# Block products for the cross terms in the second and third token groups of a GFNet + S2-MLP kernel on one Trainium2 core

## Chip, cores, metric

One core of a Trainium2 chip runs the kernel in one launch. The metric is device time in microseconds (us). The kernel before took 409.92 us, the median of three runs (409.81 to 409.93).

Engines, as the profile names them: PE (matrix products, with PEld for its weight loads), DVE (VectorE), ACT (ScalarE), POOL (GpSimd), SP (issues all transfers). Each runs its instructions in the order in which they stand in its queue, and waits there for semaphores.

## What is computed

The output is x + A(norm(x)) + B(norm(x)), for x of 2048 tokens by 448 channels:

```python
# A: spectral filter
X = rfft2(x, axes=(-2, -1))
y = irfft2(X * (w_r + 1j * w_i), s=(S, D), axes=(-2, -1))
# B: token shift, then MLP
h  = gelu(layernorm(x) @ w1)
hs = concat(shift(h[:, 0:112], +1), shift(h[:, 112:224], -1),
            shift(h[:, 224:336], +2), shift(h[:, 336:448], -2)) @ w2
x1 = x + hs
B  = x1 + gelu(layernorm(x1) @ w3) @ w4        # F = 1792 hidden channels
```

Inputs are fp32. Products run in fp16: every operand is split into a high half and a low half (the rounding rest), and a product is hi·hi + hi·lo + lo·hi.

## The kernel before

**Tiling.** The 2048 tokens are 16 blocks of 128 rows (row = 16·a + b, so a block holds every sixteenth token). The work goes through these stages, which overlap:

- layer norm of x in four groups of four blocks, `norm1`; transposes of x, partly on PE, partly as DMA transposes from SP (`turn`); w1 products (`w1_unit`, L465) and gelu; the result h goes back transposed by one DMA transpose for each block (L492) into `hT`.
- w2 products with the shifts (`w2_tile`, L510), second layer norm (`ln2`, L520), DMA transposes of its result into `x2all` (L553).
- w3 is loaded early into `w3raw` (`load_w3`, L214); its last 64 rows come once from memory and are then copied to the other 64 partitions (L1039). Sums of squares of w3 (L1043) give a power-of-two scale s3 (`powers`, with a matmul on PE at L258), and `w3_split` makes both halves.
- MLP in eight groups G = 0 to 7 of two blocks (256 tokens); a group has seven steps fp of two 128-channel slices f of the hidden layer. `front(G, fp)` (L764) makes 22 matmuls of 256 columns with w3 (L435), then the gelu on ACT (L773), the high half `hf` on ACT (L776) and the low half on DVE (L777). `back(G, fp)` (L791) multiplies by w4 into two PSUM banks `acc` (L811). `steps` (L855) interleaves them: fronts run `ahead=2` steps before backs, and cycle through the PSUM banks of `tags`, two banks to a tag.
- spectral part: `do_fold` (L571) loads x for two blocks, normalizes it on ACT and forms four sums and differences on POOL (L583, L584, L586); `step1_in` (L591) splits into halves `xh`; `step1` (L598) transforms over the rows of the block (L604). Then 16 chunks (`chunk_a`, `chunk_b`, `chunk_z`, `chunk_c`) beside G = 3 to 5, and the inverse beside G = 5 to 7.

**Block form of back.** For the groups in `STR` (G = 5, 6, 7) the cross terms hi·lo and lo·hi are not taken as whole products: the 2 × 2 blocks (two hidden slices by two token blocks for h, two slices by two column halves for w4) are multiplied in seven block products in place of eight, as in Strassen–Winograd. hi·hi stays 4 whole matmuls (L811); each of the two cross terms is 7 matmuls of 224 columns (L826). The combinations of h are made on DVE (`forms`, L786 to L788, into `hgm`), those of w4 once on POOL (`w4_forms`, L921, into `w4x`). Part of the sum lies in two more PSUM banks `cr` of tag "tr"; at the end of a group ACT copies them to `cross` (L843), and POOL (DVE for G = 7) combines (L846, L850).

**What sets the order.** A scheduler orders each engine's queue by priority and simulated readiness: `prio(EVAC)` goes first, `prio(FILL)` last. `behind(key)` pins instructions behind another on the same engine; `after[...]` keeps the keys: ("f", G, fp) is the gelu's halves, ("m", G, fp) the last matmul of a back, ("h", g, i) the transpose of h. Lists at the top pin the folds (`FOLD`, ACT behind "f"), the step1 products (`PACE`, PE behind "m"), the maxima of the spectral weights (`WMAX`, DVE, L619), and the last `ln2` (`LATE`).

**Memory that is shared.** `x2mem` holds x2all in its first 8F of 9F halves, and w4raw from 2F on to the end; `cross` is its last 896 floats and so is wsrc, and later pf_buf[1] of the chunks. The fourth buffer for folds, `xf_buf[3]`, lies in `hgm`.

Of the kernel before, what the change touches and what calls it, by code (L numbers as in the profile page):

```python
# [12 lines left out]
F32 = mybir.dt.float32  # L13
F16 = mybir.dt.float16
# [27 lines left out]

# [80 lines left out]
def body(tc, nc, x, wf, w1, w2, w3, w4, c_g, c_n, c_small, out):  # L123
# [62 lines left out]
    x2mem = pw.tile([128, 9 * F], F16, name="x2mem")  # L186
    wsrc = x2mem[:, 8 * F:8 * F + 512]
    V.memset(wsrc, 0.0)
    ones = pc.tile([128, 128], F32, name="ones")
# [36 lines left out]
    w4raw = x2mem.bitcast(F32)[:, F:].rearrange("p (f n) -> p f n", f=14)  # L226
# [293 lines left out]
    def ln2(bs, engines, pins=None):  # L520

        n, b0 = len(bs), bs[0]
        mv = stats([xb(b) for b in bs], f"b{b0}")
        a = pc.tile([128, 4], F32, tag="vb", bufs=2, name=f"vb{b0}")[:, :n]
        r = pc.tile([128, 4], F32, tag="vs", bufs=2, name=f"vs{b0}")[:, :n]
        o, y = [], []
        nm = pc.tile([128, 4], F32, tag="nm", bufs=2, name=f"nm{b0}")[:, :n]
        P.tensor_scalar(out=nm, in0=mv[:, :n, 0], scalar1=-1.0, scalar2=None, op0=ALU.mult)
        for m in range(0, n, 2):
            w = stage(f"y{b0 + m}", 8 * 448, 0 if pins else (b0 + m) // 2 % 2, F16)  # L530
            o.append(w[:, 0:4 * D].bitcast(F32).rearrange("p (i n) -> p i n", i=2))
# [12 lines left out]
        for i in range(n):
            b, h, x_ = b0 + i, y[i // 2][:, i % 2], o[i // 2][:, i % 2]
            k = r[:, i:i + 1]
            with behind("f", *pins[i]) if pins else contextlib.nullcontext():
                u = A.activation(out=h[:, 0:D], in_=x_, func=AF.Copy, scale=k)
                V.scalar_tensor_tensor(out=h[:, 448:512], in0=x_[:, 384:448], scalar=k, in1=h[:, 384:448],
                                       op0=ALU.mult, op1=ALU.subtract)  # L550
                v = V.scalar_tensor_tensor(out=h[:, 512:896], in0=x_[:, 0:384], scalar=k, in1=h[:, 0:384],
                                           op0=ALU.mult, op1=ALU.subtract)
            d = SY.dma_start_transpose(out=x2all[:, b // 4][:, :, 128 * (b % 4):128 * (b % 4) + 128], in_=h)  # L553
            after[f"b{b0}"] = u.ins, v.ins, d.ins
# [36 lines left out]
    def step1_in(b):  # L591
        f = folds.pop(b)
        t = xh_buf[b % 4]
        i = A.activation(out=t[:, 0:452], in_=f, func=AF.Copy)
        j = V.tensor_tensor(out=t[:, 452:904], in0=f, in1=t[:, 0:452], op=ALU.subtract)
        after["x", b] = i.ins, j.ins

    def step1(b):  # L598
# [192 lines left out]
    def back(G, fp):  # L791
# [47 lines left out]
        with prio(EVAC):  # L839
            if G in STR and fp == end:  # L840
                e0, e1 = cross[:, 0], cross[:, 1]
                for i in range(2):
                    A.activation(out=cross[:, i], in_=xs[G][i][:, 0:D], func=AF.Copy, scale=k34)  # L843
                for o, x, y in ((e0[:, n:], e0[:, 0:n], e0[:, n:]), (e1[:, 0:n], e1[:, 0:n], e0[:, n:]),
                                (e0[:, n:], e0[:, n:], e1[:, n:]), (e1[:, n:], e1[:, 0:n], e1[:, n:])):
                    (V if G == 7 else P).tensor_tensor(out=o, in0=x, in1=y, op=ALU.add)  # L846
            for i in range(2):
                evacuate(i)
                if G in STR and fp == end:
                    (V if G == 7 else P).tensor_tensor(out=to[i], in0=to[i], in1=cross[:, 1 - i], op=ALU.add)  # L850
                if G == 6 and fp == 6:
                    SY.dma_start(ov[:, 2 * G + i], to[i])
        yield keep(m)
# [67 lines left out]
    def w4_forms(fp):  # L921
# [4 lines left out]
        t1 = [m[:, 6], m[:, 7]]  # L926
# [7 lines left out]
        w4f[fp] += [t1] + [[x[:, i] for i in range(2)] for x in (t2, t3)]  # L934

    def squares1():
        for t in range(4):
# [165 lines left out]
    Y1 = Y.rearrange("p i q c (b k) -> p i q c b k", k=8)  # L1103
    pfd = pool("pfd", side="right")
    xf_buf = [pfd.tile([128, 2, 4, 113], F32, name=f"xf{i}") for i in range(3)]
    xf_buf.append(hgm.bitcast(F32).rearrange("p i n -> p (i n)")[:, 0:904].rearrange("p (b s d) -> p b s d", b=2, s=4))
    xh_buf = [pfd.tile([128, 2 * 452 + 16], F16, name=f"xh{i}") for i in range(4)]
    for i in range(4):
        P.memset(xh_buf[i][:, 904:], 0.0)
    mlp([1, 2], ahead=AH, tags=("mm", "tr"))  # L1110
    for b in range(0, NB, 2):
        do_fold(b)
        step1_in(b)
        step1_in(b + 1)
        with behind("m", *PACE[b // 2]):
            step1(b)
            step1(b + 1)
    with prio(FILL):
        for fp in range(7):
            with behind("fold", 0 if fp < 2 else 14):  # L1120
                w4_forms(fp)
    ln2(range(12, 16), [A] * 4, LATE)
    with behind("X", 14):
        wm = w_scale()
    close("pfd")
    with behind("m", 2, 5):
        w_scale_end(wm)
    pst = pool("pst", side="right")
    pf_buf = [pst.tile([128, 2, 2, DF], F16, name="pf0"),
# [68 lines left out]
```

## Time and profile before

| | |
|---|---|
| median of 3 runs | 409.92 us (409.81 to 409.93) |
| the profiled execution | 409.72 us |
| its span, first to last instruction | 407.6 us |
| granted PE clock | 0.999 |
| whole products of back (L811) | 508 of 448 columns, 24 of 224 |
| block products of back (L826) | 266 of 224 columns |

In the lines of the profile `out<-in` are the program's tiles, `xN` the number of instructions, then busy time and mean duration, then the idle time ahead of them with what ended it. A timeline's row starts with the start and the length in us. A row of transfers gives the size and the time from issue to landing. The row for one line of the code gives the shortest, median and longest duration in ns and the first and last start.

### The profile page before, as it was taken

The page shows a single profiled execution, that of the slowest core. Times are in us where ns is not written, and L with a number is a line of the kernel's source. Part 1 is how long each engine was busy: PE and PEld are TensorE (multiplying, and loading weights), DVE is VectorE, ACT ScalarE, POOL GpSimd, SP SyncE. Part 2 cuts the span into 40 slices and gives each one's busy share as a digit, 9 for nine tenths or more (in the row PEclk, how much of TensorE's full clock was granted, in tenths as well). Part 3 has the DMA queues.
Part 4 walks back from the last instruction along what each step waited for, and adds up shares of the span by engine and source line. Part 5 has one row for each costly group of instructions (what it writes and reads, how often), then busy time and mean ns, then how long its engine had stood idle before and what let it go on. Part 6 is the DMA issues. An engine that isn't in the chain of part 4 may idle for free.

```text
span 407.6 us, 8828 instructions
## 1 busy us (share of the span) xinstructions
PE 401.3 (98%) x3379; PEld 296.0 (73%) x3379; DVE 304.2 (75%) x658; ACT 268.6 (66%) x465; POOL 179.8 (44%) x276
## 2 busy tenths in 40 slices
PE   8998999999999999999999999999999999999996
PEld 4553555666767777776888887877788888888885
DVE  5988999899653757894577777763488879889645
ACT  4698993884737865763488888785956566544332
POOL 3889723011197747499243344441231254217100
PEclk9999999999999999999999999999999999999999
DMA  8999999915910375317055666642000022323201
GB/s 282 351 274 198 177 180 261 260 23 109 207 48 0 92 233 175 103 36 170 19 135 146 151 145 151 153 112 60 2 2 2 24 68 75 108 70 112 92 2 45
DMA packets 57209, 49.46 MB, mean 121 GB/s; under 512 B 41312, under 2 KB 52192, under 8 KB 57168
## 3 DMA queue, kind: packets, MB, share of 16 engines
q1 hardware_dynamic: 57168, 48.91, 46.4%
q8 instruction: 26, 0.43, 0.5%
q14 instruction: 15, 0.12, 0.1%
HBM read 35.06 MB, written 3.67 MB: 95 GB/s over the span
## 4 chain that ended last, share of the span: by engine, by line
PE 96%; DMA 2%; ACT 1%; DVE 0%; issue 0%; ACTq 0%
PE pw L435 33%; PE acc L811 24%; PE pw L510 9%; PE pw L465 6%; PE cr L826 4%; PE acc L826 3%; PE pu L707 3%; PE ps L604 3%; PE pp L661 2%; PE pe L727 2%; PE px L678 2%; PE py L749 2%; PE wps L889 2%; DMA h<-hs 2%; PE pta L414 1%; PE end L811 1%
## 5 line engine op out<-in xcount | busy, mean ns | idle before, releaser
L435 PE MATMUL pw<-x2mem,w3p 128*128 128x256 f16 x1232 | 149.7, 272 | 0.0
L435 PEld LDWEIGHTS <-w3p 128*128 128x128 f16 x1232 | 118.7, 98 | 19.4
L811 PE MATMUL acc<-w4p,hf 128*128 128x448 f16 x508 | 107.4, 352 | 0.0
L811 PEld LDWEIGHTS <-hf 128*128 128x128 f16 x532 | 51.5, 98 | 35.5
L777 DVE SCALAR_TENSOR_TENSOR hf<-pw,h,hf 128x512 f16<-128x512 f32 x56 | 41.8, 747 | 36.5 <-ACT hf L776 36.3
L773 ACT ACTIVATE pw<-pw,pe 128x512 f32<-128x512 f32 x56 | 36.7, 656 | 44.8 <-PE pw L435 44.6
L510 PE MATMUL pw<-w2p,h 112*128 112x448 f16 x192 | 39.2, 353 | 1.3 <-DMA h<-hs 1.2
L734 POOL TENSOR_TENSOR e<-e 128x226 f32<-128x226 f32 x16 | 11.1, 696 | 63.7 <-ACT e L731 56.2
L776 ACT ACTIVATE hf<-pw,h 128x512 f16<-128x512 f32 x56 | 38.3, 683 | 1.3
L465 PE MATMUL pw<-w1p,w4x 128*128 128x448 f16 x176 | 34.8, 352 | 0.5 <-DVE h L967 0.5
L510 PEld LDWEIGHTS <-h 112*128 112x128 f16 x192 | 18.4, 98 | 18.0 <-DMA h<-hs 2.2
L688 POOL TENSOR_TENSOR xr<-te 128x450 f32<-128x450 f32 x16 | 15.7, 981 | 34.5 <-DVE te L686 34.5
L465 PEld LDWEIGHTS <-w4x 128*128 128x128 f16 x176 | 17.1, 98 | 16.4 <-ACT w4x L424 0.7
L696 POOL TENSOR_TENSOR zb<-xr,zb 128x450 f16<-128x450 f32 x16 | 16.1, 1009 | 16.8 <-ACT zb L695 16.8
L684 DVE SCALAR_TENSOR_TENSOR te<-px,sc,wc 128x450 f32<-128x450 f32 x16 | 11.0, 685 | 10.6 <-ACT te L683 7.0
L683 ACT ACTIVATE te<-px 64x450 f32<-64x450 f32 x32 | 17.2, 538 | 1.7 <-PE px L678 1.2
L719 ACT ACTIVATE U<-y 113x512 f16<-113x512 f16 x32 | 18.0, 620 | 0.1
L741 ACT ACTIVATE vh<-e 128x448 f16<-128x448 f32 x16 | 9.2, 575 | 13.5 <-DVE e L739 13.3
L731 ACT ACTIVATE e<-pe 128x452 f32<-128x452 f32 x16 | 8.7, 545 | 14.0 <-PE pe L727 11.6
L540 POOL TENSOR_SCALAR y<-xt,nm 128x448 f32<-128x448 f32 x6 | 5.9, 986 | 23.3 <-DMA x2mem<-y 12.9
L711 DVE SCALAR_TENSOR_TENSOR y<-pu,y 113x512 f16<-113x512 f32 x16 | 10.9, 687 | 6.9 <-ACT y L710 6.8
L583 POOL TENSOR_TENSOR xr<-xf 128x452 f32<-128x452 f32 x6 | 6.7, 1125 | 20.6 <-ACT xf L579 10.5
(208 smaller groups left out, 799.0 us busy)
## 6 DMA issues: line engine op xcount, KB each, us to landing
wc<-wf SPq DMA_DIRECT2D x32, 225.0 KB, 3.8
wl<-wf SPq DMA_DIRECT2D x8, 450.0 KB, 3.9
xt<-x SPq DMA_DIRECT2D x3, 896.0 KB, 11.3
w3raw<-w SPq DMA_DIRECT2D x3, 896.0 KB, 14.6
xf<-x SPq DMA_DIRECT2D x6, 448.0 KB, 3.7
xr<-x SPq DMA_DIRECT2D x12, 224.0 KB, 2.5
out<-xr SPq DMA_DIRECT2D x12, 224.0 KB, 2.0
gn<-c_g SPq DMA_DIRECT2D x16, 128.0 KB, 3.2
```

The costliest lines, as they stand in the source:

```text
L435: m = T.matmul(ps_out, wp[:, wi + t, cols], xT[:, xi + t, tok], start=t == 0 and wi + xi == 0, stop=t == 3 and wi == 4)
L465: m = T.matmul(pm[:, :D], xTs[g][:, xi + t, 128 * i:128 * i + 128], w1p[:, wi + t], start=t == 0 and p == 0, stop=t == 3 and p == 2)
L510: m = T.matmul(w2b[b][:, :D], hT[g][:112, 4 * hi + k, o:o + 128], w2p[:, wi, k], start=k == 2 and hi + wi == 0, stop=k == 3 and hi == 1)
L683: i = A.activation(out=e[64 * h:64 * h + 64], in_=px_[64 - 64 * h:128 - 64 * h, :2 * DF], func=AF.Copy)
L688: P.tensor_tensor(out=z, in0=t[:, 0], in1=t[:, 1], op=ALU.add)
L696: P.tensor_tensor(out=zv[1], in0=z, in1=zv[0], op=ALU.subtract)
L719: A.activation(out=U[b][:113, p].rearrange("p q (c k) -> p q c k", c=NC), in_=Y1[:113, p, :, :, b], func=AF.Copy)
L773: A.activation(out=pm, in_=pm, func=AF.Gelu_apprx_tanh, scale=r3)
L776: i = A.activation(out=h[:, 0], in_=pv_, func=AF.Copy, scale=h3)
L777: j = V.scalar_tensor_tensor(out=h[:, 1], in0=pv_, scalar=h3, in1=h[:, 0], op0=ALU.mult, op1=ALU.subtract)
L811: m = T.matmul(to, h[:, hi, 2 * f + i], w4p[0][:, wi, 2 * fp + f, r], start=fp == s and f == 0 and hi + wi == 0, stop=fp == e and f == 1 a ...
L826: m = T.matmul(to, h[:, hi, slot] if slot < 4 else g[:, hi, slot - 4], w4f[fp][k][wi], start=k in (0, 6) and fp == 0 and hi == 0, stop=hi ...
```

## The change

`STR` takes in G = 1 and 2, so that `forms` and the block form of `back` run there too, and everything that stood in their way is moved:

- `w4_forms` runs on DVE (four operations a step, t1 in one), and earlier: for steps 0 to 3 behind ("f", 0, 6), for 4 to 6 behind ("f", 1, 1) to ("f", 1, 3).
- the low halves of `step1_in` run on POOL.
- fronts of G = 1 and 2 use the tag "mm" alone after the first one, since "tr" holds `cr`.
- `xf_buf[3]` moves from `hgm` to the end of `x2mem` and is used once (`FBUF`); the folds are emitted between the steps.
- the last 64 rows of w3 are loaded behind ("h", 1, 3).
- the combining at the end of groups 1 and 2 on POOL has the lowest priority.
- `PACE`, `FOLD`, `WMAX`, `LATE` change; `w_scale_end` goes behind ("m", 2, 6).

```diff
-PACE = [(0, 6), (1, 1), (1, 2), (1, 4), (1, 5), (2, 0), (2, 1), (2, 3)]
-FOLD = [(0, 5), (1, 0), (1, 1), (1, 3), (1, 4), (1, 6), (2, 0), (2, 2)]
+PACE = [(1, 0), (1, 1), (1, 2), (1, 4), (1, 5), (2, 0), (2, 1), (2, 3)]
+FOLD = [(0, 5), (0, 6), (1, 0), (1, 2), (1, 4), (1, 5), (2, 0), (2, 2)]
+FBUF = (0, 1, 2, 3, 0, 1, 2, 0)
-WMAX = [(1, 4), (1, 5), (2, 0), (2, 0), (2, 1), (2, 2), (2, 3), (2, 4)]
-LATE = [(2, 2), (2, 3), (2, 4), (2, 5)]
+WMAX = [(1, 5), (1, 6), (2, 2), (2, 3), (2, 4), (2, 4), (2, 5), (2, 5)]
+LATE = [(2, 2), (2, 3), (2, 5), (2, 6)]
-STR = (5, 6, 7)
+STR = (1, 2, 5, 6, 7)
...
-    load_w3([2, 3])
+    load_w3([2])
...
-        f = xf_buf[b0 // 2 % 4]
+        f = xf_buf[FBUF[b0 // 2]]
...
-        j = V.tensor_tensor(out=t[:, 452:904], in0=f, in1=t[:, 0:452], op=ALU.subtract)
+        j = P.tensor_tensor(out=t[:, 452:904], in0=f, in1=t[:, 0:452], op=ALU.subtract)
...
-                    (V if G == 7 else P).tensor_tensor(out=o, in0=x, in1=y, op=ALU.add)
+                with prio(EVAC if G > 2 else FILL):
+                    ...
+                        (V if G == 7 else P).tensor_tensor(out=o, in0=x, in1=y, op=ALU.add)
...
-        P.tensor_tensor(out=t3, in0=b[1][1], in1=b[0][1], op=ALU.add)
-        for i in range(2):
-            P.tensor_tensor(out=t1[i], in0=b[0][0][:, i], in1=b[0][1][:, i], op=ALU.subtract)
-            P.tensor_tensor(out=t2[:, i], in0=b[1][1][:, i], in1=t1[i], op=ALU.subtract)
-        P.tensor_tensor(out=t4, in0=b[1][0], in1=t2, op=ALU.subtract)
+        for o, x, y, op in ((t3, b[1][1], b[0][1], ALU.add), (t1, b[0][0], b[0][1], ALU.subtract),
+                            (t2, b[1][1], t1, ALU.subtract), (t4, b[1][0], t2, ALU.subtract)):
+            V.tensor_tensor(out=o, in0=x, in1=y, op=op)
...
+    with behind("h", 1, 3):
+        load_w3([3])
...
-    xf_buf.append(hgm.bitcast(F32).rearrange("p i n -> p (i n)")[:, 0:904].rearrange("p (b s d) -> p b s d", b=2, s=4))
+    xf_buf.append(x2mem.bitcast(F32)[:, 4 * F:4 * F + 904].rearrange("p (b s d) -> p b s d", b=2, s=4))
...
-    mlp([1, 2], ahead=AH, tags=("mm", "tr"))
+    gen = steps(range(1, 3), ahead=AH, tags=["tr"] + ["mm"] * 13)
+    with prio(FILL):
+        for fp in range(4):
+            with behind("f", 0, 6):
+                w4_forms(fp)
+    while ("f", 1, 3) not in after:
+        run(gen, len(slots))
+        n = len(w4f)
+        if n < 7 and ("f", 1, n - 3) in after:
+            with prio(FILL), behind("f", 1, n - 3):
+                w4_forms(n)
     for b in range(0, NB, 2):
+        while ("m", *PACE[b // 2]) not in after:
+            run(gen, len(slots))
         do_fold(b)
...
-    with prio(FILL):
-        for fp in range(7):
-            with behind("fold", 0 if fp < 2 else 14):
-                w4_forms(fp)
+    run(gen)
...
-    with behind("m", 2, 5):
+    with behind("m", 2, 6):
         w_scale_end(wm)
```

More of the change, by code (lines that the diff above doesn't have):

```diff
@@ L185, in body @@
     A.activation(out=warm, in_=warm, func=AF.Gelu_apprx_tanh)
-    x2mem = pw.tile([128, 9 * F], F16, name="x2mem")
+    x2mem = pw.tile([128, 9 * F + 16], F16, name="x2mem")
     wsrc = x2mem[:, 8 * F:8 * F + 512]
@@ L222, in body @@
     load_x(3)
-    load_w3([2, 3])
+    load_w3([2])
     cross = x2mem.bitcast(F32)[:, 4 * F:4 * F + 2 * D].rearrange("p (i n) -> p i n", i=2)
     x2all = x2mem[:, 0:8 * F].rearrange("p (j t n) -> p j t n", j=4, t=7)
-    w4raw = x2mem.bitcast(F32)[:, F:].rearrange("p (f n) -> p f n", f=14)
+    w4raw = x2mem.bitcast(F32)[:, F:9 * F // 2].rearrange("p (f n) -> p f n", f=14)
     W4F = (0, 4, 8, 11, 14)
@@ L539, in ln2 @@
                 else:
-                    e.tensor_scalar(out=o[-1][:, i], in0=xb(b0 + m + i), scalar1=1.0, scalar2=c,
-                                    op0=ALU.mult, op1=ALU.add)
+                    j = e.tensor_scalar(out=o[-1][:, i], in0=xb(b0 + m + i), scalar1=1.0, scalar2=c,
+                                        op0=ALU.mult, op1=ALU.add)
+                    after["ln", b0 + m + i] = (j.ins,)
         V.tensor_scalar(out=a, in0=mv[:, :n, 1], scalar1=eps12, scalar2=None, op0=ALU.add)
@@ L849, in back @@
                 if G in STR and fp == end:
-                    (V if G == 7 else P).tensor_tensor(out=to[i], in0=to[i], in1=cross[:, 1 - i], op=ALU.add)
+                    with prio(EVAC if G > 2 else FILL):
+                        (V if G == 7 else P).tensor_tensor(out=to[i], in0=to[i], in1=cross[:, 1 - i], op=ALU.add)
                 if G == 6 and fp == 6:
@@ L925, in w4_forms @@
         m = m.rearrange("p (k n) -> p k n", n=224)
[L926 removed]
+        t1 = m[:, 6:8]
         t2, t3, t4 = (m[:, k:k + 4:3] for k in range(3))
[L928 to L932 removed]
+        for o, x, y, op in ((t3, b[1][1], b[0][1], ALU.add), (t1, b[0][0], b[0][1], ALU.subtract),
+                            (t2, b[1][1], t1, ALU.subtract), (t4, b[1][0], t2, ALU.subtract)):
+            V.tensor_tensor(out=o, in0=x, in1=y, op=op)
         w4f[fp] = [[x[:, i] for i in range(2)] for x in (b[0][0], b[1][0], b[1][1], t4)]
[L934 removed]
+        w4f[fp] += [[x[:, i] for i in range(2)] for x in (t1, t2, t3)]
     def squares1():
```

4 lines of the change are left out of this document (2 added, 2 removed).

## The prediction

> **What bounds the kernel now.** I read the page first: the busy times, then the chain of work that ended last.
>
> ```profile
> PE 401.3 (98%) x3379; PEld 296.0 (73%) x3379; DVE 304.2 (75%) x658; ACT 268.6 (66%) x465; POOL 179.8 (44%) x276
> PE 96%; DMA 2%; ACT 1%; DVE 0%; issue 0%; ACTq 0%
> ```
>
> The span is 407.6 us and PE is busy for 401.3 of it; the chain lies on PE for 96%. Then I cut the span into stretches (busy us of PE, PEld, DVE, ACT, POOL, then clock, DMA share, GB/s).
>
> ```profile
> 0.00:32.07 32.07, 29.16 (x150) 15.55 (x151) 24.90 (x83) 20.44 (x39) 22.44 (x53) 1.00 0.99 298
> 32.07:400.00 367.93, 367.79 (x3195) 277.25 (x3196) 275.73 (x569) 246.98 (x425) 157.40 (x224) 1.00 0.43 107
> 114.20:188.70 74.50, 74.50 (x661) 56.43 (x660) 51.56 (x67) 49.49 (x88) 55.58 (x62) 1.00 0.36 103
> 301.00:370.00 69.00, 69.00 (x673) 57.91 (x672) 58.75 (x139) 38.56 (x68) 22.35 (x30) 1.00 0.18 58
> ```
>
> From 32 us to 400 us PE stands idle for 0.14 us in all, at full clock. So **less work on PE is less time**, as long as no other engine makes PE wait; and a new wait of PE anywhere there is lost one for one. Of the 2.9 us idle before 32 us, one piece matters here: PE's timeline has it just ahead of the first token mixing.
>
> ```profile
> 32.07 7.56 PE L510 MATMUL pw<-w2p,h 112*128 112x448 f16 x36 [1.17 <-DMA h<-hs]
> ```
>
> **Part 1, the products (removed from PE).** Groups 1 and 2 are 14 steps of L811, whole products: 12 matmuls of 448 columns. Groups 5 to 7 already run the block form: 4 of 448 and 14 of 224. PE's timeline of a step of each kind:
>
> ```profile
> 102.50 2.43 PE L811 MATMUL acc<-w4p,hf 128*128 128x448 f16 x12
> 104.77 2.57 PE L435 MATMUL pw<-x2mem,w3p 128*128 128x256 f16 x22
> ...
> 303.35 2.56 PE L435 MATMUL pw<-x2mem,w3p 128*128 128x256 f16 x22
> 305.75 0.92 PE L811 MATMUL acc<-w4p,hf 128*128 128x448 f16 x4
> ...
> 307.85 0.73 PE L749 MATMUL py<-vh,csm 128*128 128x448 f16 x3
> ```
>
> From start to start: whole 104.77 − 102.50 = 2.27, block 307.85 − 305.75 = 2.10. That is 0.17 saved a step, **14 × 0.17 = 2.4 us**, the largest gain in the change. The step1 products are only moved by their pins.
>
> **Part 2, the start.** Two 448 KB loads leave the first 12 us: x for the fourth fold (its buffer was hgm, free from the start; now it is the tail of x2mem, free only once w4 is split) and w3's last 64 rows (now behind the transpose of h(1,3)). DMA issues and SP's timeline:
>
> ```profile
> w3raw<-w SPq DMA_DIRECT2D x1, 448.0 KB, 18.3
> hgm<-x SPq DMA_DIRECT2D x1, 448.0 KB, 18.9
> 11.21 0.47 SPq L219 DMA_DIRECT2D w3raw<-w  x1
> 25.04 6.80 SPq L492 DMA_TRANSPOSE h<-hs  x3
> 41.57 2.66 SPq L492 DMA_TRANSPOSE h<-hs  x2
> ```
>
> The rows of w3 are issued at 11.21 and land 18.3 later, at 29.5; the x stays in flight for 18.9. The first three transposes of h meet them: 6.80 us of issue for three, against 2.66 for two later, so about 2.8 us too long. With 896 KB fewer at the 298 GB/s of that stretch the traffic ends 3.0 us sooner. PE can win at most the 1.17 us of its wait. Against that, w3's rows now come at about 44.2 (41.57 + 2.66). The nearest landing is that of their own later copy, 4.5 us; the square sums on ACT and the matmul that adds m3's sums over the partitions stand here:
>
> ```profile
> w3raw<-w3raw SPq DMA_DIRECT2D x1, 448.0 KB, 4.5
> 43.22 1.68 ACT L246 ACTIVATE xr<-w3raw 64x1792 f16<-64x1792 f32 x1
> 48.74 0.28 PE L258 MATMUL pm<-pt,ones 128*128 128x1 f32 x2
> ```
>
> 44.2 + 4.5 + 1.7 and some 0.3 for the read-out and the reduction give 50.7, so this matmul must move 2.0 us down PE's queue or PE waits 2.0; at the 18.3 of the early load it would be 15.8. Behind it wait s3 and the splits of w3 on ACT and VectorE; the copy on SP waits too, with the transposes after it. Bounds for the part: −1.2 to +2.0 (the 18.3 came at 298 GB/s of other traffic and is no guide). I take **−0.6**, half of the wait.
>
> **Part 3, VectorE in groups 1 and 2** (the stretch from 114.2 to 188.7). It loses the 16 low halves of the folds; it gains 14 × 3 forms of h and 7 × 4 forms of w4, whose durations here are (min/median/max):
>
> ```profile
> L595 DVE TENSOR_TENSOR xh<-xf,xh 128x452 f16<-128x452 f32 x12 | 11.8, 1017 | 3.1 <-ACT xh L594 3.1
> L595 DVE TENSOR_TENSOR xh<-hgm,xh 128x452 f16<-128x452 f32 x4 | 3.6, 934 | 1.0 <-ACT xh L594 1.0
> L786 DVE TENSOR_TENSOR hgm<-hf x19: 409/426/949, 291.7 to 393.0; 128x512 f16<-128x512 f16 x19
> L787 DVE TENSOR_TENSOR hgm<-hf,hgm x19: 274/283/669, 292.2 to 393.5; 128x256 f16<-128x256 f16 x19
> L788 DVE TENSOR_TENSOR hgm<-hf,hgm x19: 274/291/674, 292.5 to 393.8; 128x256 f16<-128x256 f16 x19
> ```
>
> A step's forms: 0.426 + 0.283 + 0.291 = 1.00. A form of w4 has 448 f16 elements: between the 256 of L787 (0.28) and the 512 of L786 (0.43), 0.38. So 51.56 − 15.4 + 14 × 1.00 + 28 × 0.38 = 60.8 us of 74.5. That alone fits: from 301 to 370 VectorE is at 58.75 of 69.00 and PE never waits.
>
> But these operations are held up by GpSimd. VectorE and POOL, the same low halves with POOL at work and at rest:
>
> ```profile
> 135.58 2.51 DVE L595 TENSOR_TENSOR xh<-xf,xh 128x452 f16<-128x452 f32 x2 [1.34 <-ACT xh L594]
> 135.13 1.06 POOL L583 TENSOR_TENSOR xr<-hgm 128x452 f32<-128x452 f32 x1 [0.20 <-ACT hgm L579]
> 136.15 1.45 POOL L584 TENSOR_TENSOR xr<-hgm 128x452 f32<-128x452 f32 x1
> 148.32 0.62 DVE L595 TENSOR_TENSOR xh<-xf,xh 128x452 f16<-128x452 f32 x1
> 151.82 1.07 POOL L583 TENSOR_TENSOR xr<-xf 128x452 f32<-128x452 f32 x1 [5.44 <-issue]
> ```
>
> 0.62 with POOL idle, 1.25 each with POOL busy, and POOL's own 1.06 becomes 1.45: the two take turns. POOL's load in the stretch after the change comes from these:
>
> ```profile
> L584 POOL TENSOR_TENSOR xr<-xf x6: 1056/1066/1456, 111.4 to 159.6; 128x452 f32<-128x452 f32 x6
> L586 POOL TENSOR_TENSOR xf<-xr x12: 975/983/1252, 112.5 to 162.4; 128x452 f32<-128x452 f32 x12
> L696 POOL TENSOR_TENSOR zb<-xr,zb 128x450 f16<-128x450 f32 x16 | 16.1, 1009 | 16.8 <-ACT zb L695 16.8
> L846 POOL TENSOR_TENSOR x2mem<-x2mem x8: 657/675/1101, 333.1 to 374.8; 128x224 f32<-128x224 f32 x8
> ```
>
> A fold is 2 × 1.07 + 2 × 0.98 = 4.1, seven in the stretch; 16 low halves by L696's 1.01 are 16.2; the combining at the end of group 1 is 4 × 0.68 and two of about 1.0. Together 28.7 + 16.2 + 4.7 = 49.6, a share of 0.67 (0.75 before). All 70 new VectorE operations read two tiles of SBUF, as L595 does. What each waits, from two rows:
>
> ```profile
> L786 DVE TENSOR_TENSOR hgm<-hf 128x512 f16<-128x512 f16 x19 | 9.6, 505 | 0.9
> L777 DVE SCALAR_TENSOR_TENSOR hf<-pw,h,hf 128x512 f16<-128x512 f32 x56 | 41.8, 747 | 36.5 <-ACT hf L776 36.3
> L776 ACT ACTIVATE hf<-pw,h 128x512 f16<-128x512 f32 x56 | 38.3, 683 | 1.3
> L773 ACT ACTIVATE pw<-pw,pe 128x512 f32<-128x512 f32 x56 | 36.7, 656 | 44.8 <-PE pw L435 44.6
> ```
>
> (a) The forms themselves: 0.505 − 0.409 = 0.10 at POOL's share of 22.35/69 = 0.32, so 0.20 at 0.67: 14 us, VectorE at 74.8 of 74.5. (b) The low halves: (15.4/16 − 0.62) = 0.34 at 0.75, 0.31 at 0.67: 22 us, VectorE at 82.5. What is queued behind is L777, the low half of h. PE needs it before the front two steps on (that front takes its PSUM bank: the banks go from four in turn to two). From the end of a front to that point lie 2.10 + 2.40 + 2.10 = 6.6 us, of which 0.66 + 0.68 + 0.75 go to the gelu and both halves: **4.5 us of slack**. With (a) the excess of 0.3 hides in the slack; with (b) 8.0 − 4.5 = 3.5 us come out at PE. Bounds: 0 below (VectorE was never late), and above the whole 49.6 us of POOL, 60.8 + 49.6 − 74.5 − 4.5 = 31. I take (a), the same instructions, and add **+1.0** because no queue is packed without gaps.
>
> [...]
>
> **Part 4, moved at no cost.** GpSimd drops w4's forms and gains low halves on the way to step1; it has 25 us to spare in the stretch, and four of the folds start a step earlier. w4's first forms (four groups, 6.1 us) lie behind f(0,6), where VectorE was mostly idle; without that cover they would be late for back(1,0), and come into the price of (b). w_scale_end moves one step: the scale stood ready 7 us before its first use.
>
> ```profile
> 197.17 0.15 DVE L636 TENSOR_SCALAR sc<-we 128x1 f32<-128x1 f32 x1
> 204.61 0.69 DVE L684 SCALAR_TENSOR_TENSOR te<-px,sc,wc 128x450 f32<-128x450 f32 x1 [0.36 <-DMA gn<-c_g]
> ```
>
> The second chunk's pf shares memory with group 2's combining on GpSimd (4.7 us), which may hold it up by 1 to 2 us; PE has fronts of group 3 to do meanwhile. The maxima of w and the last norms are only later, in the same stretch. Bounds 0 to 2, taken 0.
>
> **Sum.** The profiled execution took 409.72 (span 407.6 and 2.1 around it): 409.72 − 2.4 − 0.6 + 1.0 = 407.7. The median of the runs is 0.2 higher, so **407.9**.
>
> **The rivals.**
> B, slower: VectorE becomes the bound of groups 1 and 2, because its two-input operations take turns with GpSimd. It decides from an average wait of 0.26 us an operation, where 60.8 + 70 × 0.26 passes 74.5 + 4.5. With (b)'s 0.31 it costs 3.5; in rows of three and four the later ones may wait 1.25 − 0.62 = 0.6 each, 70 × 0.4 on average giving 60.8 + 28 − 79 = 9.8. Taking 5: 409.92 − 3.0 + 5 = 411.9. For it: the 1.25 above. Against it: the full stretch from 301 to 370, with PE at 69.00 of 69.00.
> C, no change: the late rows of w3 hold PE at the matmul of m3: no gain at the start, 2.0 lost, 1.0 in part 3: 409.92 − 2.4 + 2.0 + 1.0 = 410.5. For it: the rows land at 48.7 in place of 29.5. Against it: PE has other products that can go ahead.
> D, the change does not do what it says: its price in contention equals the gain of the products, or the second chunk waits 2 us: 407.9 + 2 = 409.9.
>
> **Chances.** The forecast 0.53 (its own range 406.3 to 409.0: all 1.17 won and nothing lost, 409.92 − 2.4 − 1.2 = 406.3, or nothing won at the start and 1.5 lost in part 3), B 0.33, C 0.08, D 0.06. About 0.2% (0.8 us) is what a measurement of this kernel can tell from no change. Faster by more: 0.53; within: C and D, 0.14; slower: B, 0.33. The range runs from 406.2 to 412.9: B's lower half and its middle belong to it.
>
> **What would show it.** Right: 4 + 14 matmuls in steps of 2.10 in groups 1 and 2; PE without idle time there; SP's first three transposes in about 4 us and no wait ahead of L510; L786 to L788 below 0.2 us of wait. Wrong: PE waiting for hf L777 or for xh's low half on POOL in groups 1 and 2 (B), PE waiting at L258 near 48 us (C), or at px of the second chunk near 200 us (D).

## The result and the profile after

The changed kernel takes **420.87 us** (median of 5 runs, 419.10 to 421.06); the kernel before took 409.93 us on the same chip (409.81 to 410.81). The ratio is 1.0255 [1.0233, 1.0276]: slower by 2.5%, where 407.9 us and a gain had been forecast. The profiled execution took 420.57 us, 10.85 more than that of before.

The page of the changed kernel, busy times and the shares of the chain that ended last:

```profile
PE 404.1 (97%) x3463; PEld 304.8 (73%) x3463; DVE 327.0 (78%) x712; ACT 269.6 (64%) x469; POOL 169.4 (40%) x262
PE 75%; DVE 15%; issue 3%; ACT 3%; DMA 3%; SPq 0%; DVEq 0%; ACTq 0%
```

The chain, 96% PE before, now lies for a quarter on other engines, 15% on DVE. PE has *more* busy time, although its products are less work (2.10 us a step in place of 2.27), which points to its clock. To find the place, I cut both spans at the same three points of PE's queue: the first w2 product, the first front of group 1, the first front of group 3. Before (columns as in the prediction):

```profile
32.07:116.38 84.31, 84.17 (x510) 49.58 (x511) 73.30 (x197) 65.38 (x103) 30.79 (x79) 1.00 0.79 168
116.38:192.62 76.24, 76.24 (x671) 57.38 (x670) 51.03 (x66) 49.26 (x87) 57.32 (x68) 1.00 0.40 112
```

and after:

```profile
30.68:118.51 87.83, 85.67 (x511) 50.20 (x510) 75.46 (x200) 66.31 (x106) 27.49 (x79) 0.98 0.77 167
118.51:204.45 85.94, 79.34 (x764) 66.61 (x763) 72.85 (x119) 47.92 (x86) 51.93 (x51) 0.98 0.36 101
```

The start gained 1.4 us (32.07 to 30.68), the next stretch lost 3.5 (84.31 to 87.83), groups 1 and 2 lost 9.7 (76.24 to 85.94). These 9.7 need one correction: PE has 93 matmuls more in the stretch, of which 14 × 6 = 84 are the block form's, and the rest belongs to a back of group 2 that stood behind the mark before and stands ahead of it now but for two products, 2.1 us. Without any loss the stretch would last 76.2 + 2.1 − 14 × 0.17 = 75.9 us. It **lost 10.0**.

**The first loss, at w3's late rows.** SP's timeline of the changed kernel:

```profile
24.99 4.18 SPq L493 DMA_TRANSPOSE h<-hs  x3
...
42.16 0.69 SPq L220 DMA_DIRECT2D w3raw<-w  x1
...
47.24 0.49 SPq L1043 DMA_DIRECT2D w3raw<-w3raw  x1
47.83 2.41 SPq L493 DMA_TRANSPOSE h<-x2mem  x1
```

The first three transposes take 4.18 us in place of 6.80, as expected. The rows of w3 are issued at 42.16; the copy behind them stands in SP's queue until they have landed, at 47.24, and the transposes behind it stand there too. The squares on ACT and the matmul on PE:

```profile
47.25 1.70 ACT L247 ACTIVATE xr<-w3raw 64x1792 f16<-64x1792 f32 x1 [3.46 <-DMA w3raw<-w]
```

```profile
49.28 0.38 PE L259 MATMUL pm<-pt,ones 128*128 128x1 f32 x2 [2.16 <-DVE pt L252]
```

ACT waits 3.46 for the rows, PE 2.16 for the reduction behind ACT: one delay handed on. But 2.16 does not explain 3.5. The rest is in the clock, PE's column after POOL, in these stretches of 3.41 us:

```profile
47.45:50.86 3.41, 1.58 (x10) 0.94 (x11) 1.19 (x5) 3.41 (x6) 1.79 (x9) 1.00 0.73 135
50.86:54.28 3.42, 3.42 (x11) 1.38 (x10) 3.42 (x12) 3.42 (x7) 0.00 (x0) 0.50 1.01 197
54.28:57.69 3.41, 3.41 (x20) 1.76 (x19) 3.41 (x8) 3.41 (x5) 0.00 (x0) 1.00 0.82 159
...
139.60:143.02 3.42, 0.74 (x12) 0.71 (x12) 3.42 (x7) 0.00 (x0) 1.40 (x2) 1.00 0.50 134
143.02:146.43 3.41, 3.24 (x24) 2.66 (x22) 3.38 (x9) 2.13 (x4) 0.54 (x1) 0.50 0.02 5
```

After a stretch in which PE worked for only 1.58 us, the granted clock is 0.50 for the next 3.42 us: another 1.7 us lost, while PE looks 100% busy. It happens again at 143 us.

**The second loss, at the start of group 1.** DVE:

```profile
115.59 0.75 DVE L779 SCALAR_TENSOR_TENSOR hf<-pw,h,hf 128x512 f16<-128x512 f32 x1 [3.92 <-ACT hf L778]
116.25 6.93 DVE L934 TENSOR_TENSOR w4x<-w4p 128x448 f16<-128x448 f16 x8
123.10 4.99 DVE L934 TENSOR_TENSOR w4x<-w4p,w4x 128x448 f16<-128x448 f16 x8
128.01 1.27 DVE L837 SCALAR_TENSOR_TENSOR xt<-acc,p,xt 128x448 f32<-128x448 f32 x2
129.20 0.74 DVE L779 SCALAR_TENSOR_TENSOR hf<-pw,h,hf 128x512 f16<-128x512 f32 x1
```

and the first POOL instructions beside the row of forms:

```profile
117.22 1.15 POOL L585 TENSOR_TENSOR xr<-xf 128x452 f32<-128x452 f32 x1 [0.63 <-POOL xf L588]
118.33 1.21 POOL L586 TENSOR_TENSOR xr<-xf 128x452 f32<-128x452 f32 x1
119.50 2.33 POOL L597 TENSOR_TENSOR xh<-xf,xh 128x452 f16<-128x452 f32 x2
```

Sixteen forms of w4 in a row hold DVE from 116.25 to 128.1, with the folds and the low halves on POOL for all but about 2 us of it. Behind them stand the evacuation of group 0's sums (L837) and the low half of h(1,0) (L779, at 129.20). The durations by line (min/median/max):

```profile
L934 DVE TENSOR_TENSOR w4x<-w4p x12: 373/1198/1250, 116.3 to 136.8; 128x448 f16<-128x448 f16 x12
L934 DVE TENSOR_TENSOR w4x<-w4p,w4x x12: 376/380/1230, 123.1 to 143.1; 128x448 f16<-128x448 f16 x12
```

```profile
L779 DVE SCALAR_TENSOR_TENSOR hf<-pw,h,hf x56: 735/746/752, 85.2 to 412.2; 128x512 f16<-128x512 f32 x56
```

A form takes 0.38 us alone and 1.2 beside POOL, as long as POOL's own instructions there (1.15 to 1.21): a form that follows another one waits for most of an instruction of POOL, some 0.8 us. The low half of h, L779, with one input in PSUM, keeps its 0.75 throughout: it is late only because it stands behind the row. What PE gets of it:

```profile
128.74 1.13 PE L813 MATMUL acc<-w4p,hf 128*128 128x448 f16 x4 [0.58 <-DVE xt L837]
...
131.44 0.46 PE L828 MATMUL cr<-w4x,hgm 128*128 128x224 f16 x3 [0.62 <-DVE hgm L789]
132.43 0.27 PE L828 MATMUL acc<-w4p,hgm 128*128 128x224 f16 x1 [0.53 <-DVE hgm L790]
...
139.16 0.37 PE L828 MATMUL cr<-w4x,hgm 128*128 128x224 f16 x2 [1.00 <-DVE hgm L789]
142.28 0.83 PE L606 MATMUL ps<-csm,xh 128*128 128x128 f16 x12 [2.75 <-DVE y L611]
```

All of them are waits for DVE: its evacuation, its forms of h, its low half of y (L611), which stood behind two forms of w4. The first three, 1.7 us, come right behind the row of sixteen; the last two, 3.75 us, come behind later and shorter rows of forms of w4 and h. In all PE stands idle for 85.94 − 79.34 = 6.6 us of the stretch. The second half-clock window costs 1.7 more. The last 1.7 of the 10.0 are not itemized. Part of it may lie at the breaks, since matmuls overlap in an unbroken row (a product of 448 columns is listed with 0.35 us, but 24 in a row take 4.70); this is not shown. The products themselves do what the forecast said, later in the same view:

```profile
154.08 0.92 PE L813 MATMUL acc<-w4p,hf 128*128 128x448 f16 x4
...
156.18 2.02 PE L436 MATMUL pw<-x2mem,w3p 128*128 128x256 f16 x17
```

156.18 − 154.08 = 2.10 us a step.

### The profile page after: what moved, and what is told of

Read it like the earlier page. It is cut to its first block, busy times and chain, and to the rows that moved or that the text cites. A ratio compares the mean times of both kernels' runs of the same rounds, so it can differ in the third digit from the quotient of the medians.

```text
span 418.5 us, 9086 instructions
## 1 busy us (share of the span) xinstructions
PE 404.1 (97%) x3463; PEld 304.8 (73%) x3463; DVE 327.0 (78%) x712; ACT 269.6 (64%) x469; POOL 169.4 (40%) x262
## 4 chain that ended last, share of the span: by engine, by line
PE 75%; DVE 15%; issue 3%; ACT 3%; DMA 3%; SPq 0%; DVEq 0%; ACTq 0%
PE pw L436 26%; PE acc L813 14%; PE pw L511 7%; PE cr L828 4%; PE pw L466 4%; DVE w4x L934 4%; PE acc L828 3%; PE pu L709 3%; PE pp L663 2%; PE px L680 2%; PE ps L606 2%; PE wps L893 2%; PE pe L729 2%; DVE hf L779 2%; DMA wl<-wf 1%
## 5 line engine op out<-in xcount | busy, mean ns | idle before, releaser
L436 PE MATMUL pw<-x2mem,w3p 128*128 128x256 f16 x1232 | 150.4, 273 | 0.0
L436 PEld LDWEIGHTS <-w3p 128*128 128x128 f16 x1232 | 119.4, 98 | 18.9 <-issue 0.5
L813 PE MATMUL acc<-w4p,hf 128*128 128x448 f16 x396 | 86.7, 353 | 0.6 <-DVE xt L837 0.6
L779 DVE SCALAR_TENSOR_TENSOR hf<-pw,h,hf 128x512 f16<-128x512 f32 x56 | 41.8, 746 | 28.6 <-ACT hf L778 22.8
L813 PEld LDWEIGHTS <-hf 128*128 128x128 f16 x420 | 40.5, 98 | 26.0 <-issue 1.1
L511 PE MATMUL pw<-w2p,h 112*128 112x448 f16 x192 | 40.4, 363 | 0.0
L828 PEld LDWEIGHTS <-hgm 128*128 128x128 f16 x264 | 25.0, 98 | 4.8 <-DVE hgm L789 2.9
L828 PE MATMUL cr<-w4x,hgm 128*128 128x224 f16 x174 | 25.3, 261 | 2.3 <-DVE hgm L789 2.1
L828 PEld LDWEIGHTS <-hf 128*128 128x128 f16 x198 | 18.6, 97 | 5.8 <-DVE hf L779 0.7
L788 DVE TENSOR_TENSOR hgm<-hf 128x512 f16<-128x512 f16 x33 | 19.9, 603 | 2.0 <-PE cr L828 1.1
L698 POOL TENSOR_TENSOR zb<-xr,zb 128x450 f16<-128x450 f32 x16 | 16.1, 1010 | 11.9 <-ACT zb L697 11.9
L849 POOL TENSOR_TENSOR x2mem<-x2mem 128x224 f32<-128x224 f32 x16 | 11.3, 706 | 19.9 <-ACT x2mem L845 19.1
```

The costliest lines, as they stand in the source:

```text
L436: m = T.matmul(ps_out, wp[:, wi + t, cols], xT[:, xi + t, tok], start=t == 0 and wi + xi == 0, stop=t == 3 and wi == 4)
L511: m = T.matmul(w2b[b][:, :D], hT[g][:112, 4 * hi + k, o:o + 128], w2p[:, wi, k], start=k == 2 and hi + wi == 0, stop=k == 3 and hi == 1)
L698: P.tensor_tensor(out=zv[1], in0=z, in1=zv[0], op=ALU.subtract)
L779: j = V.scalar_tensor_tensor(out=h[:, 1], in0=pv_, scalar=h3, in1=h[:, 0], op0=ALU.mult, op1=ALU.subtract)
L788: V.tensor_tensor(out=e[:, :, 0:2], in0=h[:, :, 0:3:2], in1=h[:, :, 1::-1], op=ALU.subtract)
L813: m = T.matmul(to, h[:, hi, 2 * f + i], w4p[0][:, wi, 2 * fp + f, r], start=fp == s and f == 0 and hi + wi == 0, stop=fp == e and f == 1 a ...
```

## The experiments

Theory from here on: two independent losses, (1) the late rows of w3 and (2) rows of DVE instructions that meet POOL; the half clock follows from idle time (1.83 and 2.68 us of the 3.41 ahead of it). Rivals: (1) the clock rather than the late chain binds; (2) DVE's load as such, or the low halves on POOL, rather than the rows.

### The start: w3's rows and the late x

**All of w3 loaded at the start**, x late, else as changed:

```diff
-    load_w3([2])
+    load_w3([2, 3])
...
-    with behind("h", 1, 3):
-        load_w3([3])
```

> The changed kernel with all of w3 loaded at the start again (x of the fourth fold stays late). Two stalls theory (PE waits 2.16 us for the sums of w3, then runs some 3.5 us at about half clock; groups 1 and 2 are a stall of their own): 4 us less than the changed kernel, 0.4 to 0.7 of the start's gain given back, so 416.5 to 417.5. Rival (the stages behind absorb a shift, VectorE alone sets the end): within 1 us of 420.9.

Measured 416.41 us (ratio to the kernel before, run beside it, 1.0145 [1.0107, 1.0183]). The wait at L259 and the first half-clock window are gone; most of the second loss is still there (84.50 us for the stretch in place of 85.94):

```profile
115.11:199.61 84.50, 78.85 (x763) 67.12 (x762) 73.14 (x119) 47.94 (x86) 51.90 (x51) 0.98 0.37 103
```

By the ratios, 1.0255 − 1.0145, w3's rows cost about 4.5 us.

**Only w3 late**, in the kernel before:

```diff
-    load_w3([2, 3])
+    load_w3([2])
...
+    with behind("h", 1, 3):
+        load_w3([3])
```

> The kernel before with the one edit that w3's last 64 rows load behind the transpose of h(1,3). If the late rows cost by themselves: PE waits about 2 us at the matmul of w3's sums and runs at half clock for some 3.5 us behind it, 412.5 to 414. If they cost only beside the rest of the change: within 1 us of 409.9.

Measured 413.48 us (1.0079 [1.0053, 1.0104]), as the first theory had it.

```profile
50.92 0.59 PE L258 MATMUL pm<-pt,ones 128*128 128x1 f32 x2 [3.49 <-DVE pt L251]
```

The loss stands alone in the kernel before, so it has nothing to do with the block form.

**Filling the wait**: eleven products on zeros ahead of that matmul.

```diff
-            i = T.matmul(pm[:, 0:1], ones, t, start=True, stop=True)
+            if key == "3":
+                for _ in range(11):
+                    i = T.matmul(pm, wsrc[:, 0:128], wsrc, start=True, stop=True)
...
```

> The changed kernel with 11 matmuls of 512 columns on zeros put ahead of the matmul that sums w3's squares, 2.4 us of work that nobody uses, where PE stands idle for 2.16 us. If the low clock behind that wait comes from PE standing idle: the wait itself stays, the clock stays at 1.00 between 50 and 56 us, and the time is 1.5 to 2 us shorter than the changed kernel, 419. If the clock falls for another reason: same or up to 0.5 us longer.

Measured 422.54 us (1.029 [1.0256, 1.0323]): nothing won against the changed kernel's 1.0255. The eleven ran from 46.65 to 49.02 us. PE's timeline behind them, and a stretch of 4 us:

```profile
54.77 1.69 PE L473 MATMUL pw<-w1p,w4x 128*128 128x448 f16 x8 [0.86 <-DMA w4x<-x]
```

```profile
50.00:54.00 4.00, 3.92 (x22) 1.90 (x20) 3.40 (x11) 4.00 (x9) 0.34 (x2) 1.00 0.96 180
```

The clock stays at 1.00, where the changed kernel ran at 0.50 from 50.86 to 54.28: with the wait filled it did not fall. But PE now waits at four places up to 92 us: 0.86 and 0.39 us for transposes, which stand behind w3's copy on SP, and 0.56 and 0.55 us for VectorE. These 2.4 us are more than the 1.7 that the half clock took, so the expectation of 1.5 to 2 us won was wrong. That the late chain would have taken as much without any half clock is what this points to; the fill shifts the queue as well, so it is not shown by itself.

**Only x late**, in the kernel before, with w3 early:

```diff
-    x2mem = pw.tile([128, 9 * F], F16, name="x2mem")
+    x2mem = pw.tile([128, 9 * F + 16], F16, name="x2mem")
...
-    w4raw = x2mem.bitcast(F32)[:, F:].rearrange("p (f n) -> p f n", f=14)
+    w4raw = x2mem.bitcast(F32)[:, F:9 * F // 2].rearrange("p (f n) -> p f n", f=14)
...
-    xf_buf.append(hgm.bitcast(F32).rearrange("p i n -> p (i n)")[:, 0:904].rearrange("p (b s d) -> p b s d", b=2, s=4))
+    xf_buf.append(x2mem.bitcast(F32)[:, 4 * F:4 * F + 904].rearrange("p (b s d) -> p b s d", b=2, s=4))
```

> The kernel before with the one edit that the fourth fold's buffer lies at the end of x2mem, so that its x is loaded late. If the early x was what delayed the first transposes: the first three issue in about 4 us (6.80 before), PE's wait of 1.17 us goes, 408.7 to 409.3. If w3's last rows were: no change.

Measured **407.82 us** (0.9946 [0.993, 0.9963]): faster than both kernels, and below the expected 408.7. By the ratio the gain is 2.2 us.

```profile
30.68:114.41 83.73, 83.73 (x512) 49.81 (x511) 74.14 (x198) 64.78 (x103) 31.90 (x80) 1.00 0.81 172
114.41:190.64 76.23, 76.23 (x671) 57.37 (x669) 51.01 (x66) 49.26 (x87) 57.32 (x68) 1.00 0.39 112
```

The first w2 product starts at 30.68, as in the changed kernel, with no wait ahead of it, and PE is never idle after; the first three transposes take 4.88 us. One 448 KB load fewer among the early ones gave the whole gain of the start; the second one added a loss and nothing that this shows. For the runs below that load all of w3 early and x late, 407.82 is the time without their other edits.

### VectorE beside GpSimd

The first four keep block products in groups 1 and 2.

**Low halves of the folds back on VectorE** (w3 late as in the change):

```diff
-        j = P.tensor_tensor(out=t[:, 452:904], in0=f, in1=t[:, 0:452], op=ALU.subtract)
+        j = V.tensor_tensor(out=t[:, 452:904], in0=f, in1=t[:, 0:452], op=ALU.subtract)
```

> The changed kernel with the folds' low halves back on VectorE. If taking turns with GpSimd is what delays VectorE at the start of group 1 (a form of w4 takes 1.23 us behind a GpSimd operation and 0.38 alone): GpSimd loses 16 operations that VectorE can wait for, the stall at 128 to 144 us shrinks by 2 to 4 us with the half clock behind it, 416 to 419. If VectorE's own work is the bound: 16 x 0.62 = 10 us more work on it, 424 to 430.

Measured 422.54 us (1.0287 [1.0244, 1.033]), in neither range; the interval overlaps that of the changed kernel. The stretch of groups 1 and 2 barely moves (84.72 against 85.94), and part of the wait moves to a later place (2.65 us for y, L611, ahead of 186.72). The profiled execution was late from the start (first w2 product at 32.65, in place of 30.68). Moving the low halves back, with 16 us less on GpSimd and 16 more instructions on VectorE, does not take the loss away.

The next three change the places of the rows and have all of w3 early, so compare them with 416.41.

**Folds 0 and 1 two steps earlier**: `FOLD = [(0, 3), (0, 4), (1, 0), ...`

> The kernel of e1 (all of w3 early) with the first two folds pinned earlier, FOLD (0,3) and (0,4) for (0,5) and (0,6); VectorE's work is the same. Theory (the stall at the start of group 1 comes from w4's forms meeting GpSimd's fold operations): the forms run in 0.38 us each in place of 1.23, VectorE reaches the low half of h of (1,0) some 6 us sooner, PE's idle time of 5 to 6 us in group 1 and the half clock behind it mostly go, 409 to 411.5. Rival (VectorE has too much work of its own there): no change from e1, 416.4.

Measured 413.46 us (1.0087 [1.0059, 1.0116]), between the two. The last eight of w4's sixteen forms took 2.49 us together, the two ahead of them still 2.38; the rows got shorter, and so did the loss (82.17 us for the stretch).

**w4's first forms spread**:

```diff
-        for fp in range(4):
-            with behind("f", 0, 6):
+        for fp in range(3):
+            with behind("f", 0, 5 if fp < 2 else 6):
```

> The kernel of e1 with w4's forms spread: two groups behind (0,5), one behind (0,6), the fourth behind (1,0); folds as in the change. Theory (what hurts is that the forms stand in VectorE's queue ahead of the low half of h while each waits for GpSimd): four forms fewer ahead of it and eight begun 4 us sooner, PE's idle time falls by 2 to 5 us with the half clock, 410 to 414. Rival: no change from e1, 416.4.

Measured 414.51 us (1.0092 [1.0062, 1.0122]), just above the theory's range: still one wait of 2.80 us for a form of h (L789) from 133 us on, and a granted clock of 0.96 over the stretch (115.52 to 199.10).

**Both together**:

> Both edits, the first two folds earlier and w4's forms spread, with all of w3 early. Theory: no wait of PE above 1 us in groups 1 and 2, no half clock, the products' 2.4 us are won: 407.5 to 409.5. Rival (the turns with GpSimd go on through groups 1 and 2): 411 or more.

Measured 418.32 us (1.0195 [1.0158, 1.0232]), worse than either. Earlier forms met earlier folds, and the low half of h(0,6) was now queued behind a row of eight (PE waited 2.81 us for it); the larger wait, 4.61 us for y (L611), came at 137 to 142 us:

```profile
111.85 4.74 DVE L934 TENSOR_TENSOR w4x<-w4p 128x448 f16<-128x448 f16 x4
...
119.30 0.74 DVE L779 SCALAR_TENSOR_TENSOR hf<-pw,h,hf 128x512 f16<-128x512 f32 x1
```

These three show that the place of the rows changes the time, but none removes the loss. The next ones separate the two new loads of VectorE.

**w4's forms without the block form**: all of w3 early, `STR = (5, 6, 7)`, w4's forms where the change has them.

> All of w3 loaded at the start, and STR back to (5, 6, 7): groups 1 and 2 run whole products and no forms of h, but w4's 28 forms stand on VectorE at the same places as in the change, and the low halves of the folds on GpSimd. This parts the two new loads of VectorE. If the row of w4's forms against GpSimd's folds is by itself what makes the low half of h late at the start of group 1, the idle pieces from 128 to 132 us stay, and with them perhaps a window at half clock: 411 to 414 us (407.8 of the kernel before with late x, plus 2 of idle, plus up to 1.7 of half clock). If it takes the forms of h on top of them, PE does not wait in groups 1 and 2 and the time is 407.5 to 409.

Measured 414.28 us (1.007 [1.0044, 1.0095]), just above the first theory's range and by the ratios 5.1 us more than with only x late.

```profile
114.83:196.29 81.46, 78.42 (x670) 58.45 (x668) 53.66 (x76) 47.04 (x84) 45.70 (x45) 0.98 0.37 104
```

```profile
135.14 2.56 PE L606 MATMUL ps<-csm,xh 128*128 128x128 f16 x24 [2.27 <-DVE y L611]
```

Without a single new product and without forms of h, the stretch is 5.2 us too long (81.46 against 76.24), although DVE is busy for only 53.66 of 81.46, hardly more than the 51.03 before. That settles it against VectorE's total over the stretch. In one place it is full all the same: from 112.58 to 140 us its timeline has no gap, and w4's 28 forms take 21.95 us (its rows of L934 from 112.58 on) in place of 28 × 0.38 = 10.6. With the forms of h (all of w3 early, blocks in both groups) the loss is 84.50 − 75.9 = 8.6, so 3.4 come with those in the profiled executions; by the ratios, 1.0145 − 1.007 and the 2.4 us of products won, it is 5.5.

Two things are not parted from the rows by any run. No run has the same rows with GpSimd at rest, so the share of the forms' own 10.6 us is not shown. And the fronts of groups 1 and 2 have two PSUM banks in place of four in all of these runs; PE waits ahead of no front there (L436) in the timelines of the changed kernel and of five of these runs, so no cost of it shows.

**Block products in group 2 alone**, w4's four forms of a step behind each gelu of group 1, all of w3 early:

```diff
-STR = (1, 2, 5, 6, 7)
+STR = (2, 5, 6, 7)
...
-        if n < 7 and ("f", 1, n - 3) in after:
-            with prio(FILL), behind("f", 1, n - 3):
+        if n < 7 and ("f", 1, n) in after:
+            with prio(FILL), behind("f", 1, n):
```

> All of w3 loaded at the start, block products in group 2 alone (STR without 1), and w4's forms on VectorE one step's four behind each gelu of group 1, (1,0) to (1,6), in place of sixteen in a row. Rows of VectorE forms are then four long, with no forms of h beside them in group 1. If VectorE is overloaded only where both come together, group 1 has no stall and group 2 saves 7 x 0.17 = 1.2 us: 407.8 - 1.2 = 406.6, 406 to 408. If any contention with GpSimd's folds makes PE late, group 1 still waits 2 us or more at step1 and the time is 409 to 412.

Measured 411.89 us (1.0026 [1.0003, 1.0049]), the second case, and by the ratios 3.3 us more than with only x late. VectorE and GpSimd around PE's wait of 2.29 us at 131.4 to 133.7:

```profile
128.32 2.42 DVE L934 TENSOR_TENSOR w4x<-w4p 128x448 f16<-128x448 f16 x2
130.67 2.37 DVE L934 TENSOR_TENSOR w4x<-w4p,w4x 128x448 f16<-128x448 f16 x2
132.96 0.68 DVE L611 TENSOR_TENSOR y<-ps,y 128x512 f16<-128x512 f32 x1
```

```profile
129.28 1.21 POOL L586 TENSOR_TENSOR xr<-x2mem 128x452 f32<-128x452 f32 x1
130.46 2.33 POOL L597 TENSOR_TENSOR xh<-xf,xh 128x452 f16<-128x452 f32 x2
```

A row of four forms, each 1.2 us, each in step with one POOL instruction; the low half of y behind it is late, and PE with it. Alone the four would take 4 × 0.38 = 1.5 us in place of 4.7: the 3.2 between them are more than PE's wait. No form of h was near.

**w4's forms on GpSimd, low halves on VectorE** (the engines of before, at the changed places), all of w3 early:

> All of w3 loaded at the start, block products in groups 1 and 2 as in the change, but w4's forms on GpSimd and the low halves of the folds on VectorE (the engines of the kernel before), at the changed places. If it is VectorE's row of w4 forms that holds the low half of h, the wait at 128 to 132 us goes, but GpSimd now has 28 forms of about 0.6 us or more (17 us) ahead of its folds, so the folds and with them step1 come late: a stall at L606 of some us, 412 to 418 in all. If VectorE's load were the only thing that matters, the time falls below 409.

Measured 421.87 us (1.0272 [1.0224, 1.032]).

```profile
106.42 0.95 DVE L304 TENSOR_TENSOR nqb<-nib 128x4 f32<-128x4 f32 x1
107.40 0.95 DVE L305 TENSOR_TENSOR nqb<-nqb,vb 128x4 f32<-128x4 f32 x1
...
111.55 0.74 DVE L779 SCALAR_TENSOR_TENSOR hf<-pw,h,hf 128x512 f16<-128x512 f32 x1
```

```profile
112.34 3.91 PE L813 MATMUL acc<-w4p,hf 128*128 128x448 f16 x10 [5.86 <-DVE hf L779]
```

The same thing with the roles changed: while GpSimd runs a row of forms at 1.0 us each, VectorE's norm arithmetic on 4 elements takes 0.95 us an instruction, and the low half of h behind it holds PE for 5.86 us. This stall came ahead of group 1, at a place that the expectation did not name (it had the folds late); groups 1 and 2 still took 82.76 us, 6.9 too long, and PE was busy for 78.11 of them.

**w4's forms later, where GpSimd has less to do**: as with group 2 alone, but

```diff
+W4AT = [(1, 4), (1, 5), (1, 5), (1, 6), (1, 6), (2, 0), (2, 1)]
...
-        if n < 7 and ("f", 1, n) in after:
-            with prio(FILL), behind("f", 1, n):
+        if n < 7 and ("f", *W4AT[n]) in after:
+            with prio(FILL), behind("f", *W4AT[n]):
```

> As the run with block products in group 2 alone, but w4's forms stand behind the gelus of (1,4), (1,5), (1,5), (1,6), (1,6), (2,0), (2,1), where GpSimd has 0.99 us of work in 138 to 142 us and 5.81 in 142 to 150, in place of (1,0) to (1,6), where it is busy nearly without a gap. If the wait for y at step1 (2.29 us) came from rows of w4 forms that each meet a GpSimd instruction, the wait at 131 us goes and group 2's products are won in full: 405.7 to 408 us. If it came from the mere number of VectorE instructions (43.5 us of the 76 in groups 1 and 2, with 28 x 0.38 and 21 forms of h more), a wait of 2 us or more turns up elsewhere between 138 and 190 us, where VectorE was already busy for 9.8 of 10 us: 410 to 412.

Measured 410.90 us (1.0014 [0.9992, 1.0035]); w4's forms are line 935 here.

```profile
138.69 0.68 DVE L935 TENSOR_TENSOR w4x<-w4p 128x448 f16<-128x448 f16 x2
...
145.91 4.73 DVE L935 TENSOR_TENSOR w4x<-w4p,w4x 128x448 f16<-128x448 f16 x4
```

```profile
166.11 0.54 PE L814 MATMUL acc<-w4p,hf 128*128 128x448 f16 x2 [1.84 <-DVE xt L838]
```

The wait at 131 us is gone; where GpSimd rested, two forms take 0.68 together, and where it worked, four take 4.73. But a new wait of 1.84 us at 164 to 166, for the evacuation of group 1's sums behind such forms and forms of h, took the gain of group 2. So both halves of the expectation came: the first wait went with the rows, and another came later, with the time in the range of the second case. The time without GpSimd is there (it is busy for 44.60 of the stretch's 80.50 us), but the rows in this order did not keep to it.

Against the kernel before this is no difference, but against the one with only x late (407.82) it is 2.8 us slower by the ratios. The block form in group 1 or 2 was not made to pay in any of these; whether an order exists in which it does is left open.

## Why the prediction was wrong

**Part 1 held.** Block steps in groups 1 and 2 take 2.10 us where nothing waits; the 2.4 us are in the stretch's count of work.

**Part 2, a gain and a loss that do not mix.** The prediction took −0.6 between −1.2 and +2.0. Both came true at once, each beyond its bound: the start won 1.4 us (32.07 to 30.68; with only x late the whole run wins 2.2), and the stretch behind it lost 3.5. Rival C's wait came at its named place, 2.16 us against the 2.0 worked out, with the half clock behind it. The step that failed is the reason given against C, that PE has other products to go ahead. The matmul kept its place in PE's queue, with six w2 products ahead of it (45.82) and eighteen behind (49.53), and nothing went ahead. When the wait was filled, PE waited soon after, for transposes that stood on SP behind w3's copy. The queue past which the load was moved had been named and its price left out. C's chance of 0.08 did not follow from the rows: the working itself gave 50.7 for a matmul at 48.74.

**Part 3, the term that decided.** The forecast said +1.0, rival B +5; the stretch lost 10.0, of which the run with w4's forms and no block form shows 5.2 without any form of h. The step that failed is the way of pricing, in two respects:

- *The price was an average and the wait is local.* The sum compared VectorE's total with the length of the stretch. The total came out close to case (a): 72.85 us, and 2.26 of forms ahead of the mark, are 75.1, where (a) had 74.8. Over both groups VectorE is busy for only 72.85 of 85.94 us, so no bound was reached on average. But from 116 to 150 us it is full:

```profile
116.00:150.00 34.00, 28.28 (x243) 21.42 (x241) 33.47 (x52) 16.66 (x32) 22.83 (x21) 0.95 0.15 42
```

  An engine with 13 us to spare over the stretch was held by one row for 11.9 us.
- *The wait of an operation, 0.20 from rows of forms that seldom met GpSimd, was some 0.8 in a row beside it.* The 28 forms of w4, in that same time, come to 20.15 us in place of 28 × 0.38 = 10.6, 0.34 more each:

```profile
116.00:150.00 34.00, 20.15 (x28) 0.95 0.15 42
```

  For these forms that is the size of case (b), 0.31; the prediction took (a). But (b), an average as well, would have given 3.5 us and not 10.0.

**Part 4, "moved at no cost", looked at one engine.** It put w4's first four steps (6.1 us) at a place "where VectorE was mostly idle". So it was: in the profile before, VectorE is busy for 5.27 of the 12 us from 112 to 124. But GpSimd is busy for 11.65 of them, in part with w4's forms themselves, and when these left, the second fold and the first low halves came there by the same change. The sixteen forms took 11.9 us, with the evacuation of group 0 and the low half of h(1,0) behind them; 1.7 us of PE's waits follow this row directly, and the larger ones later rows.

**Not foreseen: the half clock.** Two windows at 0.50 cost 2 × 1.7 us, though with the first of them kept at full clock (the fill) the time was no shorter. The second chunk's wait that rival D counted on did not come. Left open: 0.7 us of PE's idle, waiting for VectorE, near 387 to 389 us, in the stretch of groups 6 and 7, which the change does not touch and which some of the runs show and others not.

The account for the profiled executions: −1.4 (start) + 3.5 (w3's rows) − 2.4 (products) + 10.0 (groups 1 and 2) + 1.2 (what is left for the rest of the kernel, 0.7 of it that idle time) = +10.9; measured +10.85.

## What to carry to other kernels

In these runs a VectorE form with two SBUF inputs took as long as one GpSimd instruction when it stood in a row beside a busy GpSimd: 1.2 us in place of 0.38. A row like that is worth pricing so, and the work queued behind the row's *end* compared with its slack, not totals over a stage. When a change moves work of both engines, look whether they land beside each other. The late load cost what stood behind its dependents in the issuing queue too (0.86 and 0.39 us of PE's waits for transposes behind w3's copy, in the run with the filled wait); so one of two early loads may be worth moving and the other not: try the parts alone, as the run with only x late shows (407.82 us).

## What the runs showed of the hardware

**Stretches of 3.41 us at a clock of 0.50, behind stretches in which PE still had work.** In the changed kernel the granted clock is 0.50 from 50.86 to 54.28 us and from 143.02 to 146.43, and 1.00 between the two. In the 3.41 us ahead of them PE worked for 1.58 and 0.74 us. With group 2 alone, a stretch with 1.63 us of work was followed by full clock:

```profile
132.17:135.58 3.41, 1.63 (x25) 1.47 (x25) 3.41 (x6) 0.60 (x1) 2.73 (x3) 1.00 0.47 128
135.58:139.00 3.42, 3.42 (x30) 2.66 (x28) 2.51 (x6) 1.53 (x3) 2.20 (x2) 1.00 0.04 12
```

So a wait of 2.29 us that left 1.63 us of work in its stretch was followed by no loss of clock, and one of 2.16 that left 1.58 by a loss of 1.7 us. Two cases 0.05 us apart do not show whether the busy time decides. In the run with w4's forms on GpSimd the half clock lasted twice as long:

```profile
106.18:109.59 3.41, 0.31 (x2) 0.00 (x0) 3.27 (x6) 3.13 (x6) 3.41 (x6) 1.00 0.23 32
109.59:113.01 3.42, 0.67 (x2) 0.28 (x3) 3.42 (x6) 3.01 (x6) 1.55 (x2) 0.50 0.05 11
113.01:116.42 3.41, 3.41 (x11) 1.51 (x10) 3.41 (x6) 0.00 (x0) 2.92 (x3) 0.50 0.34 65
116.42:119.83 3.41, 3.41 (x29) 2.60 (x27) 3.37 (x4) 0.96 (x2) 3.41 (x3) 1.00 0.75 190
```

**VectorE instructions on 4 elements a partition, beside GpSimd and without it.** In the same run L304 took 0.95 us at 106.42, beside w4's forms on GpSimd; in the changed kernel the line takes 0.13 to 0.16. L309 took 0.90 at 100.34, beside the forms, and 0.15 at 112.21, in a gap of 2.36 us between GpSimd's instructions.
